# Folding the inverse features of a third pair of samples in a two-layer spectral and gated kernel, with the order of work kept as a list

## The chip, the cores and the metric

One core of a Trainium2 chip runs one program. The metric is the device time of the program in microseconds: before the change 1087.72 us, the median of 3 runs (1087.59 to 1087.82). Lower is better.

## The reference, cut to what matters

Two layers of two parts each, on x of 2048 rows (sequence) by 512 columns (features), all in single precision:

```
x = x + irfft2(rfft2(layernorm(x)) * (w_r + 1j*w_i))
n = layernorm(x)
x = x + ((n @ w_gate) * (n @ w_up)) @ w_down      # 512 -> 1792 -> 512
(the same two lines once more, with the same weights)
```

## The kernel before

**Tiling.** The 2048 rows lie as 16 tiles of 128 rows and 512 columns, called samples here (index t of `xs`). The spectral part goes in three stages: per sample the feature transform and the first part of the sequence transform (`fwd`), then the rest of the sequence transform with the filter in 16 blocks of frequencies (`middle`), then back, per sample (`inv`). The gated part (`unit`, `down`) multiplies in blocks with seven products in place of eight (names gx, gy, gw, gz, gv), each single-precision operand split into a high and a low part and multiplied in three matmuls. It reads X: the normalised, transposed samples and four sums of them, high and low (tiles xA and xS).

**The inverse and its pairs.** `inv` (L718 on) takes one sample: four twiddle products with the frequency tile E into a PSUM bank (tile vp), a ScalarE copy to SBUF (vs), the feature products with the matrix `di` into a second bank (tile yi), three VectorE additions of the bank to `xs`, and the statistics of the new row for the layer norm. In each layer the first half of the sequence goes in four pairs of samples, (0, 4), (1, 5), (2, 6), (3, 7); after each, `build_x` normalises the pair, transposes it on TensorE (tile tq) and makes X. The second half (samples 8 to 15) follows while the gated part already works on the first. The first unit of the gated part reads X of the pairs (0, 4) and (1, 5) only, the next half unit that of the other two.

**Two modes of the feature products.** In mode "plain" each of the four matmuls has 256 columns, and even and odd frequencies accumulate in the bank; the three additions read the bank as it is. In mode "fold" each matmul has 128 columns, and even and odd parts stay apart in the two halves of the bank. Then ScalarE copies the second half to SBUF (tile yb), and VectorE makes difference and sum of the halves in the bank, before the same three additions:

```
        if fold:
            yb = temp("yb", "f", (128, 256))
            act(256, lambda: A.copy(yb(), yi()[:, 256:512]), [yi], [yb])
            dve(256, lambda: tt(yi()[:, 256:512], yi()[:, 0:256], yb(), ALU.subtract), [yb], [yi])
            dve(256, lambda: tt(yi()[:, 0:256], yi()[:, 0:256], yb(), ALU.add), [yb], [yi])
```

`MODES` names the mode of each of the first half's four pairs in each layer; the second half is always folded. So 12 samples are plain and 20 folded.

**The order.** The program does not issue work as it is written. `Plan.op` records 5053 operations, each with its engine, a duration from a small cost formula, a due time and what it depends on; a tile belongs to a ring of buffers or banks. `Plan.order` then decides the order of all, which is also the order in each engine's queue: due times are carried backwards through the dependences, a scheduler (`run`) takes on each engine what is ready and due first, and a list of numbers (`MOVES`) seeds changes of due times, after each of which the order is made again from that place on. The transposed pairs use ring "d", the banks vp and yi of the pairs (2, 6) and (3, 7) and of the second half ring "a" with three banks. Engine queues run in order.

Of the kernel before, what the change touches and what calls it, by code (L numbers as in the profile page):

```python
# [26 lines left out]
def consts():  # L27
# [51 lines left out]
MODES = ("plain", "plain", "plain", "fold"), ("plain", "plain", "plain", "fold")  # L79
# [6 lines left out]
MOVES = (  # L86
# [32 lines left out]
RATE = 270.0  # L119
WARM = 2  # L120
EARLY = 0
HOLD, FAR = {"DVE": 1.0, "ACT": 1.0, "POOL": 1.0}, 15.0
CLEAR = 1.5
FREE = ("a", "f", "st", "s1", "s2", "s3")
LOOK, SLACK = 0.08, 20.0
# [23 lines left out]
class Draw:  # L149


    def __init__(self, seed):
        self.at = seed * 0x9E3779B97F4A7C15 % 2 ** 64

    def part(self):
        self.at = (self.at + 0x9E3779B97F4A7C15) % 2 ** 64
        z = self.at
        z = (z ^ z >> 30) * 0xBF58476D1CE4E5B9 % 2 ** 64
        z = (z ^ z >> 27) * 0x94D049BB133111EB % 2 ** 64
        return ((z ^ z >> 31) >> 11) * 2.0 ** -53  # L160

    def one(self, of):
        return of[int(self.part() * len(of))]

    def bell(self):
        return (self.part() + self.part() + self.part() + self.part() - 2.0) * 1.7320508


class Plan:
# [6 lines left out]
    FREE = FREE  # L176
# [31 lines left out]
    def order(self, hop=0.12):  # L208

        ops = self.ops  # L210
        for o in reversed(ops):
            d = min([ops[s]["due"] for s in o["suc"]] + [1e9 if o["due"] is None else o["due"]])
            o["due"] = d - 1.1 * o["lag"] - hop - 0.3 * (o["e"] == "PE")
        self.kinds = [(o["e"], *(t.name for t in o["tiles"])) for o in ops]
        out, marks = self.run([], [])
        for n in MOVES:
            out, marks = self.run(out, *self.move(n, out, marks)[:1])
        return out

    def move(self, n, out, marks):  # L220


        ops, draw = self.ops, Draw(n)
        end = max(o["end"] for o in out)
        lo, span = -20.0 + draw.part() * (end + 10.0), draw.one((10.0, 20.0, 40.0, 80.0, 160.0))
        share, jit, way = draw.one((0.0, 0.25, 0.5, 1.0)), draw.one((0.0, 0.0, 2.0, 5.0)), draw.part()
        inside = [o for o in ops if lo < o["start"] < lo + span]
        if way < 0.4 and inside:
            kind, by = self.kinds[draw.one(inside)["i"]], 8.0 * draw.bell()
            for o in inside:  # L230
                if self.kinds[o["i"]] == kind:
                    o["due"] += by
        elif way < 0.7 and inside:
            for _ in range(1 + int(3.0 * draw.part())):
                draw.one(inside)["due"] += 8.0 * draw.bell()
        elif inside:
            self.latest(out, end)
            shifts = sorted(o["late"] - o["due"] for o in inside)
            shift = shifts[len(shifts) // 2]
            for o in inside:  # L240
                o["due"] += share * (o["late"] - shift - o["due"]) + jit * draw.bell()
        return [m for m in marks if m[1] < lo - 15.0], lo + span

    def latest(self, out, end):
        ops = self.ops
        nxt, two = {}, None
        for o in reversed(out):
            long = o["end"] - o["start"]
            late = end - long
            for s in o["suc"]:  # L250
                late = min(late, ops[s]["late"] - (0.0 if ops[s]["next_to"] is o else long))
            if o["e"] in nxt:
                late = min(late, nxt[o["e"]] - o["pitch"])
            if o["two"]:
                if two is not None:
                    late = min(late, two - o["pitch"])
                two = late
            for t in o["tiles"]:
                if t in self.after:
                    late = min(late, self.after[t]["late"] - long)  # L260
            nxt[o["e"]] = late
            o["late"] = late

    @staticmethod
    def after_(p, o):
# [3 lines left out]
        if p["e"] != o["e"] or p["kb"]:  # L269
            return p["end"]  # L270
        return p["start"] + p["pitch"] if o["e"] == "PE" else p["end"] - 0.1

    def run(self, best, marks, pace=None, look=LOOK, hop=0.12, slack=SLACK):

        ops = self.ops
        marks = list(marks)
        m, rings, free, bus, port, after = 0, {}, {"SP": 0.75, "AQ": 0.75, "PE": 0.9, "POOL": 0.5}, 0.75, 0.0, {}
        if marks:
            m, _, rings, free, bus, port, after = marks[-1]
# [28 lines left out]
        while len(out) < len(ops):  # L308
            nexts = []
# [967 lines left out]
```

## Time and profile before

| | before |
|---|---|
| median of 3 runs | 1087.72 us |
| the profiled execution | 1087.75 us |
| its span, first to last instruction | 1086.0 us |
| TensorE busy | 1072.3 us (99%) |
| VectorE busy | 841.1 us (77%) |
| ScalarE busy | 457.7 us (42%) |
| GpSimd busy | 731.8 us (67%) |
| granted TensorE clock | 1.00 |

The profile records one execution. Busy time is the time in which an engine had an instruction under way; the ends of matmuls are modelled, and the times of consecutive ones overlap, so the distance from start to start says what one takes. All recorded work of the kernel's helpers has one line (L411), so instructions are told apart by their tiles. A granted clock of 1.00 is TensorE's full clock.

### The profile page before, as it was taken

The numbers are of one execution on the slowest core, as the hardware profiler recorded it, in microseconds if no ns is written. First come the engines' busy times: TensorE is split into PE (matmuls) and PEld (weight loads), VectorE is DVE, ScalarE is ACT, GpSimd is POOL, SyncE is SP. The second block draws the span as 40 slices with busy tenths as digits, with TensorE's granted clock in tenths as the row PEclk, the third lists the DMA queues.
The fourth block names the chain that finished last, engine by engine and source line by source line (L and its number), as shares of the span: only waits on it lengthen the run. The fifth ranks groups of instructions, "written<-read, shape, count | busy, mean of one in ns | idle before, by whom it ended". The sixth has DMA issues, their size and how long they took to land.

```text
span 1086.0 us, 18629 instructions
## 1 busy us (share of the span) xinstructions
PE 1072.3 (99%) x6500; PEld 923.2 (85%) x6500; DVE 841.1 (77%) x1684; ACT 457.7 (42%) x1045; POOL 731.8 (67%) x940
## 2 busy tenths in 40 slices
PE   8999999999999999999999999999999999999998
PEld 6748988888899988888996489889989998888887
DVE  8597877777877875766897979777897876677778
ACT  6787643344542323323347775223442521223231
POOL 7396799978898666456674527466656984667771
PEclk9999999999999999999999999999999999999999
DMA  7665267556563457454454312655456256556542
GB/s 282 234 213 175 64 223 242 199 204 203 214 223 117 166 182 235 155 165 147 136 199 151 136 54 103 207 168 180 155 175 204 69 175 242 186 184 203 194 137 78
DMA packets 50301, 189.49 MB, mean 174 GB/s; under 512 B 5280, under 2 KB 19104, under 8 KB 39200
## 3 DMA queue, kind: packets, MB, share of 16 engines
q0 software_dynamic: 16128, 102.77, 28.8%
q1 hardware_dynamic: 33792, 85.01, 22.2%
q8 instruction: 52, 0.85, 0.3%
q10 hardware_dynamic: 288, 0.52, 0.1%
q14 instruction: 41, 0.34, 0.1%
HBM read 145.56 MB, written 42.73 MB: 173 GB/s over the span
## 4 chain that ended last, share of the span: by engine, by line
PE 89%; DVE 5%; issue 2%; ACT 2%; POOL 1%; DMA 0%; DVEq 0%; POOLq 0%; ACTq 0%
PE gx L411 14%; PE gz L411 14%; PE db L411 7%; PE gw L411 7%; PE gv L411 7%; PE gy L411 7%; PE ex L411 5%; PE ez L411 5%; PE yi L411 3%; PE ey L411 3%; PE ew L411 3%; PE ev L411 3%; PE sp L411 2%; PE dp L411 2%; PE vp L411 2%
## 5 line engine op out<-in xcount | busy, mean ns | idle before, releaser
L411 PE MATMUL gx<-xA,wt 128*128 128x512 f32 (+1 forms) x852 | 180.8, 347 | 0.0
L411 PEld LDWEIGHTS gx<-xA,wt 128*128 128x128 f32 x852 | 136.9, 190 | 17.2 <-ACT s L411 0.2
L411 DVE TENSOR_TENSOR q<-gy,s 128x512 f32<-128x512 f32 (+1 forms) x71 | 41.1, 578 | 73.4 <-PE gy L411 55.9
L411 ACT CAST sf<-q 128x256 fp32r<-128x256 f32 x99 | 40.2, 406 | 136.5 <-DVE q L411 84.0
L411 POOL TENSOR_TENSOR sf<-q,sf 128x256 fp32r<-128x256 f32 x99 | 73.6, 745 | 31.8 <-ACT sf L411 28.1
L411 DVE TENSOR_TENSOR xs<-xs,db 128x512 f32<-128x512 f32 x128 | 85.6, 683 | 11.4 <-PE db L411 11.0
L411 PE MATMUL db<-wd,h 128*128 128x512 f32 x336 | 91.1, 395 | 0.0
L411 POOL DMA_DIRECT2D wt<-gu x72 | 40.3, 560 | 74.7 <-PE gz L411 48.1
L411 PE MATMUL gz<-xA,wt 128*128 128x512 f32 (+1 forms) x426 | 90.1, 347 | 0.0
L411 PE MATMUL gw<-xS,wt 128*128 128x512 f32 (+1 forms) x426 | 90.0, 347 | 0.0
L411 PE MATMUL gv<-xS,wt 128*128 128x512 f32 (+1 forms) x426 | 90.0, 347 | 0.0
L411 PE MATMUL gz<-xS,wt 128*128 128x512 f32 (+1 forms) x426 | 89.8, 346 | 0.0
L411 PE MATMUL gy<-xS,wt 128*128 128x512 f32 (+1 forms) x426 | 89.7, 346 | 0.0
L411 POOL TENSOR_TENSOR sf<-cc,sf 128x256 fp32r<-128x256 f32 x99 | 73.2, 740 | 21.1 <-ACT sf L411 20.7
L411 PEld LDWEIGHTS gz<-xA,wt 128*128 128x128 f32 x426 | 69.1, 189 | 9.4
L411 PEld LDWEIGHTS gw<-xS,wt 128*128 128x128 f32 x426 | 68.8, 189 | 9.3 <-issue 0.3
L411 PEld LDWEIGHTS gy<-xS,wt 128*128 128x128 f32 x426 | 68.7, 190 | 9.0 <-issue 0.3
L411 PEld LDWEIGHTS gz<-xS,wt 128*128 128x128 f32 x426 | 68.8, 190 | 8.9
L411 PEld LDWEIGHTS gv<-xS,wt 128*128 128x128 f32 x426 | 68.5, 190 | 8.9 <-issue 0.3
L411 ACT COPY s<-gx 128x512 f32<-128x512 f32 (+1 forms) x71 | 35.3, 497 | 92.7 <-PE gx L411 80.7
L411 PEld LDWEIGHTS db<-wd,h 128*128 128x128 f32 x336 | 60.3, 189 | 10.3
L411 ACT CAST sf<-cc 128x256 fp32r<-128x256 f32 x99 | 40.1, 405 | 66.4 <-PE ez L411 22.3
(171 smaller groups left out, 2667.1 us busy)
## 6 DMA issues: line engine op xcount, KB each, us to landing
wt<-gu POOLq DMA_DIRECT2D x36, 1024.0 KB, 5.3
wt<-gu POOLq DMA_DIRECT2D x36, 768.0 KB, 4.7
bf<-dn POOLq DMA_DIRECT2D x20, 1024.0 KB, 5.5
bf<-dn POOLq DMA_DIRECT2D x20, 768.0 KB, 4.6
gu<-wt SPq DMA_DIRECT2D x14, 1024.0 KB, 6.9
gu<-wt SPq DMA_DIRECT2D x14, 768.0 KB, 3.5
wq<-in_wf_dram SPq DMA_DIRECT2D x10, 1024.0 KB, 6.1
rg<-in_wb_dram SPq DMA_DIRECT2D x14, 512.0 KB, 4.8
```

Source lines behind the costliest of these rows:

```text
L411: ins = f(*args, **kw)
```

## The change

In both layers the pair (2, 6) goes from "plain" to "fold", as (3, 7) already is: in four samples the four feature matmuls have 128 in place of 256 columns, and one ScalarE copy and two VectorE operations are added. That makes 12 operations more, 5065 in all.

The search for an order no longer runs when the program is built: `Draw`, `move`, `latest` and `run` go, and `order` takes the operations as a list of their numbers, `ORDER`, says, keeping the bookkeeping of buffers and banks. The list was searched anew, so the order differs in many places over the whole program, not only where pairs are folded.

```diff
-MODES = ("plain", "plain", "plain", "fold"), ("plain", "plain", "plain", "fold")
+MODES = ("plain", "plain", "fold", "fold"), ("plain", "plain", "fold", "fold")
...
+ORDER = (
...
+    572, 321, 583, 530, 681, 505, 323, 519, 324, 531, 584, 325, 326, 585, 586, 506, 327, 573, 587, 328, 532, 588, 590,
+    533, 589, 329, 534, 518, 591, 535, 574, 695, 623, 696, 520, 575, 638, 538, 536, 576, 697, 637, 577, 521, 537, 578,
+    592, 539, 593, 639, 597, 598, 682, 599, 594, 595, 683, 602, 596, 522, 698, 600, 523, 603, 524, 684, 601, 525, 699,
+    330, 640, 606, 700, 604, 526, 624, 701, 607, 540, 625, 613, 331, 641, 609, 541, 608, 642, 545, 626, 546, 547, 610,
+    542, 615, 543, 544, 550, 685, 643, 616, 702, 548, 551, 611, 644, 686, 862, 849, 554, 703, 612, 617, 687, 619, 555,
+    618, 605, 688, 621, 561, 704, 620, 689, 553, 627, 705, 562, 645, 500, 690, 511, 501, 502, 706, 708, 622, 741, 646,
+    514, 628, 883, 614, 707, 515, 629, 549, 691, 647, 1040, 512, 709, 516, 630, 863, 552, 556, 513, 650, 850, 557, 648,
+    565, 559, 851, 649, 896, 566, 864, 631, 563, 742, 852, 651, 564, 692, 853, 558, 743, 632, 567, 560, 744, 865, 693,
+    568, 633, 710, 747, 634, 711, 854, 745, 884, 635, 746, 885, 652, 715, 653, 748, 716, 717, 657, 886, 658, 659, 750,
+    720, 654, 655, 749, 866, 656, 662, 712, 751, 721, 713, 752, 917, 714, 753, 660, 855, 856, 718, 768, 857, 1093, 769,
...
+    3135, 3070, 3136, 3081, 3137, 3138, 3139, 3082, 3083, 3244, 3140, 3071, 3245, 3084, 3231, 3072, 3141, 3085, 3246,
+    3232, 3422, 3087, 3073, 3086, 3074, 3247, 3469, 3142, 3075, 3233, 3088, 3189, 3146, 3143, 3089, 3147, 3148, 3248,
+    3144, 3090, 3145, 3173, 3249, 3151, 3094, 3174, 3091, 3190, 3095, 3096, 3152, 3250, 3149, 3191, 3456, 3092, 3192,
+    3175, 3150, 3093, 3155, 3251, 3156, 3234, 3193, 3157, 3158, 3153, 3252, 3194, 3235, 3159, 3164, 3253, 3154, 3236,
+    3160, 3176, 3168, 3195, 3254, 3162, 3161, 3436, 3166, 3237, 3177, 3437, 3165, 3163, 3255, 3099, 3238, 3167, 3170,
+    3178, 3100, 3097, 3239, 3169, 3179, 3103, 3240, 3098, 3171, 3196, 3180, 3423, 3104, 3101, 3424, 3181, 3110, 3105,
+    3102, 3182, 3425, 3111, 3106, 3197, 3457, 3108, 3256, 3292, 3107, 3112, 3199, 3293, 3198, 3257, 3258, 3113, 3109,
+    3183, 3114, 3426, 3438, 3115, 3200, 3116, 3184, 3241, 3295, 3201, 3202, 3117, 3427, 3439, 3242, 3206, 3203, 3294,
...
-        self.kinds = [(o["e"], *(t.name for t in o["tiles"])) for o in ops]
-        out, marks = self.run([], [])
-        for n in MOVES:
-            out, marks = self.run(out, *self.move(n, out, marks)[:1])
-        return out
...
+        for o in (ops[n] for n in ORDER):
+            e = o["e"]
+            at = max([self.after_(ops[p], o) for p in o["pre"]] + [free.get(e, 0.75), port if o["two"] else 0.0])
...
                     if len(q) == self.RINGS.get(t.ring, 1):
                         old = min((u for u in q if not u.left), key=lambda u: u.freed)
-                        after[old] = o
+                        at = max(at, old.freed)
                         q.remove(old)
```

The numbers count the operations in the order in which the program makes them. Layer 0, the first lines of the list shown: 698, 640, 685 and 627 are the feature products of samples 7, 6, 3 and 2; 641 to 643 and 628 to 630 are copy, difference and sum that folding adds for samples 6 and 2; 603 and 601, 551 and 549 are the transposes of the pairs (1, 5) and (0, 4); 741 and 742 are the first two products of the gated part, gw and gx; 850 and 851, 863 and 864 are the twiddle products of samples 8 and 12, and 853 the feature products of sample 8; 705 to 707 and 647 to 649 are ScalarE's statistics of samples 7 and 6. Layer 1, the second lines: 3189 are the feature products of sample 6; 3292 and 3293 are gw and gx, and 3457 is one of the twiddle products of sample 9, the other of which comes later.

## Rows read from the trace of the kernel before

**Rows 1.** Busy time of each engine, its share of the span, and instructions.
```profile
PE 1072.3 (99%) x6500; PEld 923.2 (85%) x6500; DVE 841.1 (77%) x1684; ACT 457.7 (42%) x1045; POOL 731.8 (67%) x940
```

**Rows 2.** Windows: length, busy us (instructions) of each engine, clock, DMA share, GB/s.
```profile
0.00:50.00 50.00, 45.33 (x335) 35.41 (x336) 33.37 (x107) 33.45 (x87) 24.91 (x39) 1.00 0.76 271
50.00:86.00 36.00, 34.89 (x92) 15.64 (x91) 35.07 (x63) 28.93 (x54) 32.80 (x32) 1.00 0.56 196
...
92.00:116.00 24.00, 22.41 (x162) 20.71 (x162) 20.96 (x73) 21.53 (x61) 11.76 (x16) 1.00 0.41 149
98.00:110.00 12.00, 10.41 (x73) 9.22 (x73) 11.33 (x36) 11.41 (x32) 6.03 (x9) 1.00 0.63 229
140.00:260.00 120.00, 120.00 (x569) 100.63 (x568) 91.34 (x172) 47.80 (x94) 104.81 (x110) 1.00 0.66 228
...
630.00:654.00 24.00, 22.90 (x164) 21.18 (x162) 21.38 (x73) 20.71 (x59) 8.55 (x12) 1.00 0.13 39
636.00:648.00 12.00, 10.90 (x74) 9.57 (x73) 11.12 (x35) 10.34 (x29) 4.60 (x7) 1.00 0.08 23
980.00:1086.00 106.00, 101.89 (x610) 90.24 (x608) 80.31 (x129) 27.10 (x63) 61.30 (x86) 1.00 0.47 155
```

**Rows 3.** Chain that ended last: start us, us, engine, tile, instructions.
```profile
0.75 3.82 DMA xs<-in_x_dram
...
91.56 1.73 PE yi L411 x8
...
105.84 1.23 ACT sq L411 x4
...
107.76 0.71 ACT sq L411 x2
...
114.19 0.89 PE yi L411 x8
...
647.07 2.38 PE vp L411 x20
...
1080.67 1.28 DVE xs L411 x2
```

**Rows 4.** Groups by shape: count | busy us, mean ns | idle before.
```profile
L411 DVE TENSOR_TENSOR xs<-xs,yi 128x256 f32<-128x256 f32 x64 | 25.3, 414 | 0.3
...
L411 DVE TENSOR_TENSOR xs<-xs,yi 128x512 f32<-128x512 f32 x32 | 21.9, 683 | 9.7 <-PE yi L411 9.3
...
L411 DVE TENSOR_TENSOR yi<-yi,yb 128x256 f32<-128x256 f32 x40 | 17.0, 428 | 3.9 <-ACT yb L411 3.2
...
L411 ACT COPY yb<-yi 128x256 f32<-128x256 f32 x20 | 7.5, 377 | 8.0 <-PE yi L411 5.1 <-POOL u L411 1.2 <-POOL h L411 0.9
...
L411 ACT CAST xS<-sx 128x256 fp32r<-128x256 f32 x16 | 6.2, 408 | 0.9 <-DVE sx L411 0.7 <-POOL sx L411 0.2
```

**Rows 5.** Who waited for tile yb: us, times.
```profile
  DVE yi L411: 3.2, 4
```

**Rows 6.** TensorE's waits, whole span: us in total, times, longest us.
```profile
PE tq L411 <- ACT xn L411: 1.6, 2, 1.2
...
PE yi L411 <- ACT vs L411: 1.1, 2, 0.7
```

**Rows 7.** Timeline of TensorE in layer 0: start, us, tile, shape, count, idle before.
```profile
106.80 2.04 PE L411 MATMUL vp<-tw,E 128*128 128x128 f32 x16
108.67 0.60 PE L411 MATMUL tq<-ident,xn 128*128 128x128 f32 x4
109.71 1.16 PE L411 MATMUL yi<-di,vs 128*128 128x128 f32 x8 [0.43 <-ACT vs L411]
110.62 0.96 PE L411 MATMUL gw<-xS,wt 128*128 128x256 f32 x6
```

**Rows 8.** Timeline of GpSimd in layer 0.
```profile
106.85 3.51 POOL L411 TENSOR_TENSOR xS<-sx,xS 128x256 fp32r<-128x256 f32 x5
```

**Rows 9.** Timeline of TensorE in layer 1.
```profile
649.21 0.96 PE L411 MATMUL gx<-xA,wt 128*128 128x256 f32 x6
```

More of the change, by code (lines that the diff above doesn't have):

```diff
@@ L85 @@
 ON_POOL = range(16), range(16)
-MOVES = (
[32 rows of a table removed]
+ORDER = (
[257 rows of a table added]
 RATE = 270.0
@@ L121 @@
 EARLY = 0
-HOLD, FAR = {"DVE": 1.0, "ACT": 1.0, "POOL": 1.0}, 15.0
 CLEAR = 1.5
-FREE = ("a", "f", "st", "s1", "s2", "s3")
-LOOK, SLACK = 0.08, 20.0
 SLOTS = 5
@@ L146, in __call__ @@
         return self.tile
[L149 to L166, printed above, removed]
 class Plan:
@@ L174 @@
              **{f"{r}{p}": n for p in range(4) for r, n in (("s", SLOTS),)}}
-    FREE = FREE
     def __init__(self):
@@ L208, in order @@
     def order(self, hop=0.12):
-        ops = self.ops
+        ops, out, rings, free, bus, port = self.ops, [], {}, {}, 0.75, 0.0
         for o in reversed(ops):
@@ L213, in order @@
             o["due"] = d - 1.1 * o["lag"] - hop - 0.3 * (o["e"] == "PE")
-        self.kinds = [(o["e"], *(t.name for t in o["tiles"])) for o in ops]
-        out, marks = self.run([], [])
-        for n in MOVES:
-            out, marks = self.run(out, *self.move(n, out, marks)[:1])
-        return out
[L220 to L262, printed above, removed]
+        for o in ops:
+            for t in o["tiles"]:
+                t.left, t.slot, t.freed = t.users, None, 0.0
@@ new lines, in order @@
+        for o in (ops[n] for n in ORDER):
+            e = o["e"]
+            at = max([self.after_(ops[p], o) for p in o["pre"]] + [free.get(e, 0.75), port if o["two"] else 0.0])
+            if e == "SP":
+                at = max(at, o["due"] - o["ahead"])
+            for t in o["tiles"]:
+                if t.slot is None:
+                    t.slot = True
+                    q = rings.setdefault(t.ring, [])
+                    t.index = len(q)
+                    if len(q) == self.RINGS.get(t.ring, 1):
+                        old = min((u for u in q if not u.left), key=lambda u: u.freed)
+                        at = max(at, old.freed)
+                        q.remove(old)
+                        t.index = old.index
+                    q.append(t)
+            o["start"] = at
+            free[e] = at + o["pitch"]
+            if o["two"]:
+                port = at + o["pitch"]
+            if o["kb"]:
+                bus = max(bus, at) + o["kb"] / RATE
+                o["end"] = max(at + o["lag"], bus + 2.3)
+            else:
+                o["end"] = at + o["lag"] + hop + 0.3 * (e == "PE")
+            for t in o["tiles"]:
+                t.left -= 1
+                t.freed = max(t.freed, o["end"])
+            out.append(o)
@@ L271, in after_ @@
         return p["start"] + p["pitch"] if o["e"] == "PE" else p["end"] - 0.1
[L273 to L279, printed above, removed]
-        rings, free, after, out = {g: list(q) for g, q in rings.items()}, dict(free), dict(after), best[:m]
-        done, mark = sum(o["e"] == "PE" for o in out), marks[-1][1] if marks else 0.0
-        ready, turn = {}, {}
-        for o in ops:
-            o["n"], o["out"] = len(o["pre"]), False
-            for t in o["tiles"]:
-                t.left, t.slot, t.freed, t.due = t.users, None, 0.0, None
-        for o in out:
-            o["out"] = True
-            for s in o["suc"]:
-                ops[s]["n"] -= 1
-            for t in o["tiles"]:
-                t.left -= 1
-                t.slot, t.freed = True, max(t.freed, o["end"])
-        for o in sorted(ops, key=lambda o: (o["due"], o["i"])):
-            for t in o["tiles"]:
-                if t.due is None:
-                    t.due = o["due"]
-                    if t.slot is None:
-                        turn.setdefault(t.ring, []).append(t)
-        def enter(o):
-            o["at"] = max([self.after_(ops[p], o) for p in o["pre"]], default=0.0)
-            ready.setdefault(o["e"], []).append(o)
-        for o in ops:
-            if not o["n"] and not o["out"]:
-                enter(o)
-        while len(out) < len(ops):
-            nexts = []
-            for e, cand in sorted(ready.items(), key=lambda r: free.get(r[0], 0.0)):
-                if nexts and free.get(e, 0.0) > min(a for a, _ in nexts) + look:
-                    break
-                can = []
-                for o in cand:
-                    at = max(o["at"], free.get(e, 0.0), port if o["two"] else 0.0)
-                    if e == "SP":
-                        at = max(at, o["due"] - o["ahead"])
-                    want, early = {}, False
-                    for t in o["tiles"]:
-                        if t.slot is None:
-                            early = early or t.due > turn[t.ring][0].due + (slack if t.ring in self.FREE else 0.0)
-                            want[t.ring] = want.get(t.ring, 0) + 1
-                    if early:
-                        continue
-                    for g, n in want.items():
-                        when = sorted(t.freed for t in rings.get(g, ()) if not t.left)
-                        n -= self.RINGS.get(g, 1) - len(rings.get(g, ()))
-                        at = max(at, 1e9 if n > len(when) else when[n - 1] if n > 0 else 0.0)
-                    if at < 1e9:
-                        can.append((at, o))
-                if can:
-                    first = min(a for a, _ in can)
-                    take = min(((a, o) for a, o in can if a <= first + look), key=lambda c: (c[1]["due"], c[1]["i"]))
-                    if e in HOLD:
-                        soon = [(a, o) for a, o in can if a < take[0] + HOLD[e] * take[1]["pitch"] and o["due"] < take[1]["due"] - FAR]
-                        take = min(soon, key=lambda c: (c[1]["due"], c[1]["i"]), default=take)
-                    nexts.append(take)
-            if not nexts:
-                raise AssertionError([(o["e"], o["i"], [t.ring for t in o["tiles"]]) for c in ready.values() for o in c][:40])
-            first = min(a for a, _ in nexts)
-            if first > mark + 20.0:
-                mark = first
-                marks.append((len(out), first, {g: list(q) for g, q in rings.items()}, dict(free), bus, port, dict(after)))
-            at, o = min((c for c in nexts if c[0] <= first + look), key=lambda c: (c[1]["due"], c[1]["i"]))
-            if o["e"] == "PE":
-                assert not pace or at < pace[done]
-                done += 1
-            ready[o["e"]].remove(o)
-            for t in o["tiles"]:
-                if t.slot is None:
-                    t.slot = True
-                    q = rings.setdefault(t.ring, [])
-                    t.index = len(q)
-                    if len(q) == self.RINGS.get(t.ring, 1):
-                        old = min((u for u in q if not u.left), key=lambda u: u.freed)
-                        after[old] = o
-                        q.remove(old)
-                        t.index = old.index
-                    q.append(t)
-                    turn[t.ring].remove(t)
-            o["start"] = at
-            free[o["e"]] = at + o["pitch"]
-            if o["two"]:
-                port = at + o["pitch"]
-            if o["kb"]:
-                bus = max(bus, at) + o["kb"] / RATE
-                o["end"] = max(at + o["lag"], bus + 2.3)
-            else:
-                o["end"] = at + o["lag"] + hop + 0.3 * (o["e"] == "PE")
-            for t in o["tiles"]:
-                t.left -= 1
-                t.freed = max(t.freed, o["end"])
-            out.append(o)
-            for s in o["suc"]:
-                ops[s]["n"] -= 1
-                if not ops[s]["n"]:
-                    enter(ops[s])
-        self.after, self.marks = after, marks
-        return out, marks
```

271 rows, old and new, of tables (MOVES, ORDER) are left out of this document.

## Prediction, made before the changed kernel was run

> **What bounds the kernel now.** I read the profile in five views: engine totals, windows by stage, the chain that ended last, TensorE's waits, and timelines of the two places that the change touches.
>
> TensorE is busy 1072.3 of 1086.0 us [rows 1]: 13.7 us of idleness in all. The windows place it [rows 2]: 4.67 us in the first 50 us, 1.11 in 50 to 86, 1.59 in 92 to 116, 1.10 in 630 to 654, 4.11 in the last 106, about 1.1 over the rest. In the long gated stage (140 to 260 stands for the others) it is never idle. So whatever TensorE no longer has to do shortens the program, but only where it would not then stand still instead. The granted clock is 1.00 in every window, TensorE's upper level of 2.4 GHz, so the clock is no term here.
>
> The change sits in the two stretches where that condition is in doubt. In 98 to 110 us TensorE is busy 10.41 of 12 us, VectorE 11.33 and ScalarE 11.41; in 636 to 648 it is 10.90, 11.12 and 10.34 [rows 2]. The chain there runs over ScalarE's statistics [rows 3] and comes back to TensorE at 109.71 us, where TensorE stood still for ScalarE's copy [rows 7]. TensorE's waits for a normalised row (1.2 and 0.4 us) and for that copy (0.7 and 0.4) all lie in these two stretches [rows 6]. Locally, VectorE and ScalarE set the pace, and TensorE is kept going with work of the second half of the sequence, pulled forward.
>
> The profiled execution took 1087.75 us, 1.75 outside its span; the median of the runs is 1087.72. I sum on the profiled one and take the difference over to the median as it is.
>
> **The fold on TensorE.** The plain features of a sample are eight instructions in 1.73 us, the folded ones eight in 0.89 [rows 3]. Four samples change (6 and 2, in each layer): 4 x 0.84 = 3.36 us less TensorE work. This is the only large term with a sure sign.
>
> **What the fold adds.** Per sample one ScalarE copy of 377 ns and two VectorE operations of 428 ns [rows 4]: per layer 0.75 us on ScalarE and 4 x 0.428 = 1.71 on VectorE. What would hide them is free time on these engines. In 92 to 116 VectorE has 24 - 20.96 = 3.04 us free, ScalarE 2.47; in 630 to 654 it is 2.62 and 3.29 [rows 2]. By these rows they fit. But in the inner 12 us VectorE has only 0.67 and 0.88 us free, ScalarE 0.59 and 1.66, and the added operations have to run in there, ahead of or among the operations that build X for the first product. Cost from both sides: nothing if the free time takes all, 2 x 1.71 = +3.42 us if all stands on the path to X.
>
> The fold also adds a wait: VectorE's difference needs ScalarE's copy, and behind it on VectorE queue the additions to xs and the small scale operations that ScalarE's normalisation waits for. The existing 20 folded samples paid 3.2 us in 4 waits for such a copy [rows 5]: 0.8 us when it happens, so 0 to 3.2 us for four. I take nothing of its own for it, since it falls into the same VectorE time as the term above. The bank of the features stays occupied longer by copy and two operations, 0.38 + 0.86, less the 0.84 that the features are shorter: 0.4 us a sample, 0 to 1.6 in all. I take 0, because the list lets other samples' work come between.
>
> **The order.** The list can be read directly, since it numbers the operations as the program makes them. In layer 0 the first product gw (741) now stands ahead of the twiddle products of samples 8 and 12 (850, 851, 863, 864), the features of sample 8 (853) and the second transpose of pair 0 (549). Before, all of these ran ahead of it: 108.67 - 106.80 = 1.87, 110.62 - 109.71 = 0.91, and 0.60 us [rows 7]. With 1.68 us saved, TensorE comes to gw 5.06 us earlier, if nothing else holds it. What holds it is X. The last low part that gw reads is the fourth of five GpSimd operations that begin at 106.85 and take 3.51 us, so it was ready near 106.85 + 4 x 0.70 = 109.65 [rows 8]. On ScalarE statistics of samples 7 and 6 (1.23 and 0.71 us in the chain, [rows 3]) go behind the cast that this part needs, against one copy and one cast more ahead of it (0.38 and 0.41, [rows 4]): 1.94 - 0.79 = 1.15 us earlier. On VectorE four operations of 256 columns and one of 512 leave (4 x 0.42 + 0.68), two fold operations enter (0.86): 1.5 us earlier. The smaller holds: X near 108.5, so gw near 108.5 instead of 110.62, while 1.87 + 0.91 + 0.60 = 3.38 us of moved work is still to be done: 3.4 - 2.1 = +1.3 us. The other end is that X follows TensorE fully: -1.68. I take +0.4: the moved work can stand in waits behind gw, where X for gx is not ready yet, but the row on X is the nearer one.
>
> In layer 1 TensorE reached gx (649.21) without a wait [rows 9], after five twiddle products of the second half, 2.38 us in the chain [rows 3]. Now one of the five, some 0.48 us, comes behind gx, so TensorE is there 2.16 us earlier. VectorE has 1.71 us more ahead of X and the list moves little of its work back. Ends: -1.68 if free time takes all; +1.71 if X comes that much later. I take -0.4: VectorE's 2.62 us free in this stretch exceed the addition, but only 0.88 of them lie in the inner 12 us.
>
> The rest of the list differs from the old order by a few places nearly everywhere. In the gated stages there is no idle time to win. In the head (4.67) most is the first load, 3.82 us in the chain [rows 3]. The tail's 4.11 us end in a VectorE chain, its last pair of additions 1.28 us [rows 3], and the list leaves the last five VectorE operations as they were. Between -2.0 and +1.0; I take -0.7, half of the idle time in 50 to 86 and a little of the tail.
>
> **Sum:** +0.4 - 0.4 - 0.7 = -0.7 us; the saving of 3.36 is inside the first two terms. 1087.72 - 0.7 = 1087.0 us.
>
> A rule of the Trainium skill bears on this: "Perfetto Trace Analysis", section "Identifying the Most-Contended Engine", says that matmul busy time misleads, that weight-load time should be read instead, and that the engine with the highest occupancy is the one to relieve. In 98 to 110 us weight loads take 9.22 of 12 us, below VectorE and ScalarE [rows 2], so by that rule this change relieves the wrong engine in its own stretch; it is the slower rival below. The rows bear it out for the inner 12 us, not for the program, where TensorE stands above both.
>
> **Rivals.**
> (a) X follows. VectorE's free time takes the additions, TensorE waits no longer than before, and all of the 3.36 us is kept. For it: both stretches have more free time on VectorE than is added. Against: the inner windows. Time: 1087.72 - 3.36 - 0.7 = 1083.7 us; with a third lost, 1084.8.
> (b) VectorE becomes the bound; the slower side. Eight added operations stand ahead of X, TensorE's saving turns into waiting for the first product, and the time grows by up to 3.42 us. It decides from the point where the additions exceed the 0.67 and 0.88 us of the inner windows, which leaves 3.42 - 1.55 = +1.9 at least. For it: the inner windows and the chain over ScalarE. Against: the list defers the statistics of samples 6 and 7. Time: +3.42 - 0.7 gives 1090.4 us; from 1089.6 on.
> (c) The new order decides and the fold does not matter: head, tail and the two spectral stages move by more than 2 us. It needs idle time that the windows show only at both ends; its times lie within the range and I give it no case of its own.
>
> **How the numbers follow.** About 0.2% (2.2 us) is what a measurement of this kernel can tell from no change: 1085.5 to 1089.9. My forecast, most of the saving given back as waits, 0.47, with its own range 1085.6 to 1088.9. Rival (a) 0.35: a real removal on the engine that bounds the program, and my hand count of X may be late by more than 1 us. Rival (b) 0.18. Faster 0.35, same 0.47, slower 0.18. Range: 1083.9, where most of (a) is inside, to 1089.9, where the lighter half of (b) ends; both tails together leave out about 0.2.
>
> **What would show it.** Right: features of 128 columns 192 instead of 160, TensorE busy some 3 us less, and its idle time in the two stretches larger by 2 to 4 us, in front of gw in layer 0 and gx in layer 1. The difference's wait for the copy would show as VectorE idle before the fold. For (a): idle in 92 to 116 and 630 to 654 stays near 1.59 and 1.10. For (b): VectorE over 95% from the first addition to the first product and the gated stage starting later than 110.6 and 649.2 us. I am wrong if the time is outside 1085.5 to 1089.9, or if the head or tail moves by more than 2 us.

## The result, and the profile after

The changed kernel takes 1091.17 us (median of 7 runs, 1090.04 to 1092.71) against 1087.82 us for the kernel before beside it (7 runs, 1087.26 to 1088.80): ratio 1.003, 95% interval 1.0019 to 1.0041. It is 3.3 us slower. I had forecast 1087.0, and 1083.9 to 1089.9 as the range.

The profiled execution took 1090.87 us, its span 1089.1. Engine totals, in the columns of [rows 1]:

```profile
PE 1070.4 (98%) x6500; PEld 921.9 (85%) x6500; DVE 846.2 (78%) x1692; ACT 458.7 (42%) x1049; POOL 732.6 (67%) x940
```

TensorE is busy 1.9 us less and VectorE 5.1 us more. So TensorE stands idle 18.7 us instead of 13.7. The windows, in the columns of [rows 2]; the first, 92 to 116, 98 to 110, 630 to 654 and 636 to 648 answer to rows there:

```profile
0.00:50.00 50.00, 46.23 (x336) 35.32 (x337) 32.15 (x108) 34.56 (x87) 24.63 (x39) 1.00 0.75 262
92.00:116.00 24.00, 20.59 (x162) 19.31 (x161) 22.04 (x72) 21.79 (x63) 11.01 (x15) 1.00 0.50 176
98.00:110.00 12.00, 8.89 (x71) 8.01 (x69) 11.19 (x35) 11.48 (x35) 8.13 (x12) 1.00 0.54 183
630.00:654.00 24.00, 21.15 (x152) 19.38 (x151) 21.97 (x70) 19.67 (x58) 8.42 (x12) 1.00 0.13 38
636.00:648.00 12.00, 10.06 (x79) 9.10 (x77) 11.60 (x41) 11.40 (x33) 4.93 (x7) 1.00 0.12 37
```

TensorE's idle time in 92 to 116 is 24 - 20.59 = 3.41 us (1.59 before), in 630 to 654 it is 2.85 (1.10 before): together +3.57, against 3.36 us of work saved. So the two stretches gain next to nothing, as the prediction had it; how much of the +3.57 is the fold's is told by e2 below. The features by shape, in the columns of [rows 4], and TensorE's waits as in [rows 6]:

```profile
L488 PE MATMUL yi<-di,vs 128*128 128x128 f32 x192 | 25.6, 277 | 4.0 <-DVE xs L488 3.3 <-ACT vs L488 0.7
L488 PE MATMUL yi<-di,vs 128*128 128x256 f32 x64 | 14.6, 379 | 0.0
```
```profile
PE yi L488 <- DVE xs L488: 3.3, 2, 2.1
...
PE ez L488 <- DVE xs L488: 0.9, 1, 0.9
...
PE ew L488 <- DVE xs L488: 0.2, 1, 0.2
```

192 features have 128 columns, as announced. Two kinds of wait are new: a features step for VectorE's additions to xs (2.10 and 1.21 us), since they hold the bank of ring "a" that it needs; and ez and ew for such additions. The first sits here, in TensorE's timeline of layer 0 (columns as in [rows 7]):

```profile
101.37 1.16 PE L488 MATMUL yi<-di,vs 128*128 128x128 f32 x8 [0.68 <-ACT vs L488]
102.39 0.66 PE L488 MATMUL tq<-ident,xn 128*128 128x128 f32 x4
105.14 1.16 PE L488 MATMUL yi<-di,vs 128*128 128x128 f32 x8 [2.10 <-DVE xs L488]
106.05 0.96 PE L488 MATMUL gw<-xS,wt 128*128 128x256 f32 x6
107.12 0.66 PE L488 MATMUL tq<-ident,xn 128*128 128x128 f32 x4
107.61 2.05 PE L488 MATMUL vp<-tw,E 128*128 128x128 f32 x16
109.42 0.36 PE L488 MATMUL gx<-xA,wt 128*128 128x256 f32 x1
110.29 0.86 PE L488 MATMUL gx<-xA,wt 128*128 128x256 f32 x5 [0.51 <-DVE xA L488]
...
651.05 0.96 PE L488 MATMUL gw<-xS,wt 128*128 128x256 f32 x6
```

gw starts at 106.05 instead of 110.62 [rows 7], sooner than the 108.5 that I had worked out for X, but the stall came before it and the moved work (transpose and twiddle products) still follows. In layer 1 (last row) the first product starts at 651.05 instead of 649.21 [rows 9].

That leaves most of the 3.3 us outside the two stretches, where the prediction had expected a small gain. Part of it shows as idle time at the end of layer 0's gated stage with the forward transform of layer 1 (550 to 600 us, called the handover below), and part in the gated stage of layer 1. Before, then after:

```profile
550.00:570.00 20.00, 20.00 (x165) 18.85 (x163) 19.05 (x48) 10.09 (x26) 15.10 (x22) 1.00 0.60 218
570.00:600.00 30.00, 29.16 (x182) 20.00 (x181) 22.73 (x55) 21.74 (x50) 15.68 (x19) 1.00 0.47 169
700.00:980.00 280.00, 280.00 (x1792) 254.68 (x1792) 215.60 (x387) 91.72 (x207) 183.35 (x256) 1.00 0.53 172
```
```profile
550.00:570.00 20.00, 19.80 (x163) 18.51 (x161) 17.97 (x42) 8.20 (x22) 12.78 (x18) 1.00 0.61 219
570.00:600.00 30.00, 28.30 (x187) 20.61 (x186) 23.19 (x56) 22.05 (x53) 15.16 (x19) 1.00 0.43 146
700.00:980.00 280.00, 279.23 (x1781) 253.39 (x1780) 217.69 (x388) 91.02 (x205) 183.06 (x254) 1.00 0.53 173
```

TensorE is idle 1.90 us in the handover instead of 0.84, and 0.77 instead of 0 in 700 to 980.

### The profile page after: what moved, and what is told of

The parts are those of the page before. It is cut to its first block, busy times and chain, and to the rows that moved or that the text cites. A ratio compares the mean times of both kernels' runs of the same rounds, so it can differ in the third digit from the quotient of the medians.

```text
span 1089.1 us, 18628 instructions
## 1 busy us (share of the span) xinstructions
PE 1070.4 (98%) x6500; PEld 921.9 (85%) x6500; DVE 846.2 (78%) x1692; ACT 458.7 (42%) x1049; POOL 732.6 (67%) x940
## 4 chain that ended last, share of the span: by engine, by line
PE 91%; DVE 3%; ACT 2%; DMA 2%; issue 1%; POOL 0%; POOLq 0%; DVEq 0%
PE gx L488 14%; PE gz L488 14%; PE db L488 8%; PE gy L488 7%; PE gv L488 7%; PE gw L488 7%; PE ez L488 5%; PE ex L488 5%; PE yp L488 3%; PE dp L488 3%; PE sp L488 3%; PE yi L488 3%; PE ev L488 3%; PE ey L488 2%; PE ew L488 2%; PE zp L488 2%
## 5 line engine op out<-in xcount | busy, mean ns | idle before, releaser
L488 PEld LDWEIGHTS gx<-xA,wt 128*128 128x128 f32 x852 | 137.9, 190 | 18.7 <-DVE xA L488 0.9
L488 POOL TENSOR_TENSOR sf<-q,sf 128x256 fp32r<-128x256 f32 x94 | 70.1, 746 | 36.0 <-ACT sf L488 34.8
```

Of the source, the lines that this page charges most:

```text
L488: ins = f(*args, **kw)
```

## The experiments

The theories. BANK: the wait for the bank in ring "a" is the cost. VECTOR: VectorE's added work is the cost, whichever buffer shows it. ORDER: the newly searched order is slower by itself, with or without the fold; PLACE says its loss has places that add up, SPREAD that it hasn't. CLOCK: TensorE's granted clock falls behind a stall. "Old order" is the kernel before's, written as a list; every median is given against the median of the kernel before, measured beside it, with the 95% interval of the ratio.

**e1, e2: order and fold taken apart.** e1 is the old order with the fold, e2 the new order without it:

```diff
-MODES = ("plain", "plain", "fold", "fold"), ("plain", "plain", "fold", "fold")
+MODES = ("plain", "plain", "plain", "fold"), ("plain", "plain", "plain", "fold")   # e2
 ORDER = (
...   # e1: old order, per sample copy + difference + sum put in; e2: new order less these twelve
```

> The order of the kernel before, kept as a list, with the third pair folded in both layers: each copy stands behind its features, each difference and sum ahead of the first addition; everything else is as before. Theory BANK (the features of samples 6 and 2 wait for a bank of ring a, which VectorE's longer additions hold; 2.10 and 1.21 us in the profile after): the fold itself costs, so this is no faster than before, 1087 to 1090. Theory VECTOR (the added 3.4 us of VectorE work are served ahead of what TensorE needs next, whichever buffer shows it): the same 1087 to 1090, the idle of 92 to 116 and 630 to 654 about 3 us above before. Theory ORDER (the fold gives its 3.4 us or nearly, and the newly searched order loses about 6 elsewhere): 1084 to 1086.

> The order of the changed kernel with its twelve added instructions taken out, and the third pair's features plain as before. Theory ORDER: the order is what is slower, so this is 1091 or, with the TensorE work back, up to 1094. Theories BANK and VECTOR: the order costs what the idle outside the two stretches shows, about 1.4 us, so 1088 to 1090.

Measured: e1 1093.29 (+5.6; ratio 1.0040 to 1.0065), e2 1091.19 (+3.5; 1.0020 to 1.0045). e2 is the changed kernel's time without the fold in it: on the new order the fold nets 0.0 us, to within some 1.8 us by the two intervals, and the order alone is 3.5 us slower. ORDER holds for the changed kernel. The two stretches in e2's profile, and its wait for the bank, as in [rows 2] and [rows 6]:

```profile
92.00:116.00 24.00, 21.37 (x156) 19.88 (x155) 20.52 (x66) 20.94 (x58) 10.72 (x15) 1.00 0.50 176
630.00:654.00 24.00, 22.52 (x151) 20.59 (x151) 20.88 (x64) 18.88 (x55) 8.27 (x12) 1.00 0.13 39
PE yi L488 <- DVE xs L488: 1.8, 1, 1.8
```

TensorE is idle 2.63 + 1.48 = 4.11 us there, so 1.42 of the +3.57 us come with the order and 2.15 with the fold, and most of the longer wait for the bank is there without the fold.

On the old order the fold costs far more than any theory had for it: the ranges ended at 1090. The twelve operations were put into that order by hand, each copy right behind its features, and VectorE's queue then stands still for the copy, in e1's timeline of layer 0:

```profile
104.78 0.90 DVE L489 TENSOR_TENSOR yi<-yi,yb 128x256 f32<-128x256 f32 x2 [1.45 <-ACT yb L489]
```

In all VectorE waits for the copy 4.9 us in 6 cases in e1, against 3.2 in 4 before and 0.9 in 2 in the changed kernel. An order searched from the old one for the fold was not run, so e1's price is that of this placement.

**e3, e4: the new order, the added work out, or the bank wait out.**

```diff
-        if fold:
+        if fold and t not in (2, 6):     # e3
             yb = temp("yb", "f", (128, 256))
-... if k < 2 else ("a", "a"),
+... if k < 2 else ("a", {7: "y", 3: "x"}.get(t, "a")),     # e4
```

> The changed kernel with the third pair's features folded but its copy, difference and sum left out (the added features of samples 2, 3's partner 6, of both layers are then not put together; what is left out is four copies, four differences, four sums). Theory VECTOR: the work was the price, the time falls by 2.5 to 4 us to 1087 to 1088.5. Theory BANK: the additions start earlier, so the wait for the bank goes as well, the same 1087 to 1088.5. Theory ORDER: the added work hardly matters, 1090 to 1091.

> The changed kernel with the same order and work, but the features of samples 7 and 3 (the fourth pair) in the banks y and x, which lie idle there, so that ring a has a free bank when the features of 6 and 2 come up. Theory BANK: the waits of 2.10 and 1.21 us go and the time falls by 2 to 3.3 us, to 1088 to 1089. Theory VECTOR: TensorE starts the features earlier and waits as long a little later, for the transposes or the first products; time within 1 us of 1091. Theory ORDER: as VECTOR.

(In e3 the samples meant are 2 and 6.) Measured: e3 1089.31 (+1.6; 1.0004 to 1.0021), 1.9 under the changed kernel and between the ranges of VECTOR and ORDER; e4 1091.70 (+4.0; 1.0025 to 1.0047). In e4 TensorE's timeline shows the bank wait gone and others in its place:

```profile
102.30 0.66 PE L489 MATMUL tq<-ident,xn 128*128 128x128 f32 x4 [0.80 <-ACT xn L489]
102.79 1.06 PE L489 MATMUL yi<-di,vs 128*128 128x128 f32 x8
105.02 0.38 PE L489 MATMUL gw<-xS,wt 128*128 128x256 f32 x1 [1.18 <-ACT xS L489]
106.01 0.85 PE L489 MATMUL gw<-xS,wt 128*128 128x256 f32 x5 [0.60 <-POOL xS L489]
```

The features of sample 2 no longer wait (102.79); TensorE waits 0.80 us for a normalised row ahead of them and 1.18 + 0.60 us for X behind them. In the two stretches TensorE is busy 21.24 and 20.76 of 24 us, so idle 6.0 us, against 6.3 in the changed kernel. BANK falls by these rows; VECTOR's "waits as long a little later" is what they show. The time alone would not settle it, since in e4's profile the granted clock of 92 to 116 is 0.93, and 1.00 in the changed kernel's. e3's gain of 1.9 us, under its expected 2.5 to 4, is the price of the added ScalarE and VectorE work on the new order, and the change's profit on TensorE there is as large (e3 is also 1.9 under e2).

**e5, e6, e7: the two halves of the fold, on the old order.** e5 issues the third pair's folded features twice, so only the added work is left; e6 leaves the added work out; e7 unfolds the fourth pair too.

```diff
-            for i in range(4):
+            for i in (*range(4), *(range(4) if t in (2, 6) else ())):     # e5
```

> The kernel of e1_old_order_fold with each folded features matmul of the third pair issued twice (the same result), so that TensorE's 3.4 us come back and only the added work of ScalarE and VectorE is left as the change. Theory VECTOR: in the two stretches TensorE waits for VectorE anyway, so the 3.4 us fall into its idle time: not slower than e1's 1093.3. Theory CLOCK (e1's profile has TensorE at half clock in 106 to 112 and 650 to 654, right behind its idle time, some 3.4 us of lost work; with TensorE busier the clock stays): faster than e1 although TensorE does more, 1089.5 to 1091.5. If TensorE's saving was real in e1: 1096 to 1097.

> The order of the kernel before, the third pair's features folded, but without the copies, differences and sums (the added features of samples 2 and 6 are then not put together): TensorE's saving alone. Theory VECTOR: without VectorE's added work the saving shows, at most 3.4 us, 1085 to 1087. Theory CLOCK: VectorE's old work already sets the pace, the saved time becomes idle and the clock falls behind it: 1087.5 to 1090. If the saving counts in full: 1084.3.

> The order of the kernel before with the fourth pair's features plain as well (four copies, four differences and four sums fewer, TensorE +3.4 us). Theory VECTOR: before has 2.7 us of idle TensorE time in the two stretches, and VectorE's additions end earlier, so at most 1 to 2.5 us are lost or nothing: 1087.5 to 1090. If TensorE is what counts there: 1091.

Measured: e5 1094.15 (+6.35; 1.0046 to 1.0071), e6 1087.89 (+0.1; 0.9990 to 1.0008), e7 1089.89 (+2.1; 1.0010 to 1.0027). For e5 both VECTOR and CLOCK had expected no more than 1093.3, and the count in full 1096: all miss. e6 lies in CLOCK's range, e7 in VECTOR's. The windows tell why; 92 to 116 and 630 to 654 in e1, e5 and e6, columns as in [rows 2], the clock third from the end:

```profile
92.00:116.00 24.00, 19.22 (x136) 18.23 (x135) 19.75 (x64) 19.84 (x56) 11.24 (x15) 0.93 0.42 149
630.00:654.00 24.00, 20.57 (x132) 18.94 (x131) 19.92 (x60) 17.31 (x47) 5.49 (x8) 0.93 0.15 46
```
```profile
92.00:116.00 24.00, 20.65 (x144) 19.95 (x144) 18.49 (x58) 18.30 (x51) 9.75 (x14) 0.86 0.41 148
630.00:654.00 24.00, 21.49 (x153) 19.89 (x151) 19.02 (x58) 17.31 (x47) 5.02 (x7) 1.00 0.17 49
```
```profile
92.00:116.00 24.00, 21.99 (x162) 21.13 (x161) 20.93 (x73) 21.50 (x61) 11.56 (x16) 0.93 0.40 149
630.00:654.00 24.00, 21.50 (x161) 20.14 (x161) 21.34 (x72) 20.20 (x59) 8.55 (x12) 1.00 0.13 39
```

A granted clock below 1.00 over 24 us is lost work that busy time hides: (1 - 0.93) x 24 = 1.7 us. With it, three terms from each profile (TensorE's work, its idle time in the two stretches against before's 1.59 + 1.10, the lost work) come near the times, all in us:

| | work | idle | clock | sum | measured |
|---|---|---|---|---|---|
| e1 fold | -3.4 | +5.5 | +3.4 | +5.5 | +5.6 |
| e5 added work only | 0 | +3.2 | +3.4 | +6.5 | +6.35 |
| e6 TensorE's saving only | -3.4 | +1.8 | +1.7 | +0.1 | +0.1 |
| e7 nothing folded | +3.4 | -0.8 | 0 | +2.6 | +2.1 |
| e9 (below) | +5.0 | -0.4 | 0 | +4.7 | +4.8 |

The sums are a reading and not a measurement: each takes the windows of one execution, and they leave out the first 50 us, where e1's clock is 0.97 and its TensorE 1.1 us less idle. For e6 the clock's term is too large: three of its eleven executions have a mean clock of 1.00 and take 1086.96 to 1087.73, the other eight (0.997 and 0.998) 1087.47 to 1088.25, medians only 0.4 apart. So where the clock stays up, most of its 1.7 us seems to be waited instead.

So on the old order TensorE's saving is worth nothing that can be told even when VectorE pays nothing for it (e6), and the added work, 3.4 us on VectorE, costs 6.3 (e5). Near half of that price fits the wait for the copy: in e5's profile VectorE waits for it 6.7 us in 6 cases, 3.5 more than before. The fourth pair's fold, which before has already, is worth 2.1 (e7): the first fold pays, the second doesn't. What fits, and was not tested, is that VectorE had room for the first (busy 8.63 of 12 us in 98 to 110 in e7) and has little for the second (11.33 before).

**e9: the stalls filled.** Thirteen matmuls that nobody reads, where TensorE waited in e1:

```diff
+    def keep_busy(wz, m):
+        for _ in range(m):
+            TE.matmul(wz()[:, 0:384], ident, midt, start=True, stop=True, skip_group_check=True)
```

> The kernel of e1_old_order_fold (1093.3) with thirteen matmuls of 128x384 that nobody reads, put ahead of the instructions for which TensorE waited in its profile: four and four in layer 0 (waits of 2.00 and 2.25 us), one, three and one in layer 1 (0.54, 1.54, 0.67). Theory CLOCK: TensorE stays at the full granted clock behind them, and the lost work of about 1.7 us in 106 to 112 and 1.7 us in 650 to 654 comes back: 1089 to 1091.5, faster although TensorE does 5 us more. Rival VECTOR ALONE: VectorE's and ScalarE's results come when they come and the clock costs nothing that they don't hide: 1093 to 1095.

Measured: 1092.56 (1092.33 to 1092.67), 0.7 under e1 (1092.61 to 1093.46), not the 2 to 4 us of the expectation, and under the rival's 1093 to 1095 as well. TensorE's windows of 2 us in e1 and then in e9 (length, busy us (instructions), clock, DMA share, GB/s):

```profile
106.00:108.00 2.00, 0.55 (x2) 0.88 1.05 435
108.00:110.00 2.00, 2.00 (x12) 0.50 0.73 307
110.00:112.00 2.00, 2.00 (x15) 0.77 0.00 0
...
650.00:652.00 2.00, 2.00 (x11) 0.56 0.00 0
652.00:654.00 2.00, 2.00 (x13) 0.59 0.16 48
```
```profile
106.00:108.00 2.00, 2.00 (x10) 1.00 1.03 432
108.00:110.00 2.00, 2.00 (x20) 1.00 0.50 209
110.00:112.00 2.00, 1.57 (x14) 1.00 0.03 8
...
650.00:652.00 2.00, 1.40 (x13) 1.00 0.05 12
652.00:654.00 2.00, 2.00 (x19) 1.00 0.30 93
```

In e1 the clock is at 0.50 (1.2 GHz) behind the stalls; in e9 it stays at 1.00 (2.4 GHz). The gain is small because the fillers were too long. Eight records of them run from 102.05 to the next step at 104.63, so 26 take 26/8 x 2.58 = 8.4 us, while the idle time fell by only 8.2 - 2.3 = 5.9. 8.4 - 5.9 less 3.4 of clock is -0.9, near the -0.7. More TensorE work made the kernel a little faster, as CLOCK says; the number in the expectation rested on the fillers' wrong length.

**e8, e10 to e14: where the new order loses.** All plain, spliced from both orders:

```diff
 ORDER = (
...   # e8: new to place 450, then old; e10: new to 800; e13: new to 2250
...   # e11: new in 2250 to 2880, else old; e12: old to 2880, then new; e14: old in 2250 to 2880, else new
```

Behind a seam the second order goes on with what has not been issued yet.

> Plain third pair; the order of the changed kernel up to the end of the filter stage of layer 0 (the first 450 places of the list), then that of the kernel before. In the profiles the new order reaches the first inverse twiddle after the filter 0.5 to 1.0 us sooner (84.5 to 85.0 us against 85.5) and loses later, in the stretches and at the handover near 570 us. Theory ORDER-PLACE: the head's gain stays and the losses go: 1086.7 to 1087.2. Rival: the second half of the head's gain is lost again in the first stretch, which waits for ScalarE and VectorE: 1087.7.

> Plain third pair; the changed kernel's order for the first 800 places (to behind the stretch of layer 0), then that of the kernel before. Theory PLACE (the new order's loss of 3.4 us in e2 is the sum of its idle time: stretch 0 about 1.0, handover 570 about 1.1, stretch 1 about 0.9, the rest in the gated stage of layer 1): head -0.4 and stretch +1.0, so 1088 to 1089. Rival: the loss lies in this part whole: 1091.

> Plain third pair; the order of the kernel before, with the changed kernel's order in places 2250 to 2880 (the end of layer 0's gated stage and the forward transform of layer 1, where TensorE waits 0.20 and 0.86 us for VectorE's xs near 567 and 572 us in the new order and not in the old). Theory PLACE: 1088.5 to 1089. Rival: the waits there are made up at the filter stage, which VectorE bounds: 1087.7.

> Plain third pair; the order of the kernel before for the first 2880 places, then the changed kernel's (filter of layer 1, its stretch, its gated stage and the end). Theory PLACE: +0.9 for the stretch and up to 1 for waits on loads in the gated stage (0.4 us twice in the profile of the changed kernel, none before): 1088.5 to 1089.8, with a wider spread than before's. Rival: the loss of 3.4 us lies here whole, since only here the two orders' executions differ in spread: 1091.

> Plain third pair; the changed kernel's order for the first 2250 places (all of layer 0 but the end of its gated stage), then that of the kernel before; at that place both have issued the same operations. Theory PLACE (the parts of e2's 3.4 us add up: handover 1.8, from filter 1 on 0.7, so 0.9 is left for layer 0): 1088.3 to 1089.2. Rival SPREAD (no one place: loads that come late by chance of phase, in any mixture with the new beginning): 1090 to 1091 with a spread over 2 us, as e10.

> Plain third pair; the changed kernel's order but for places 2250 to 2880 (the handover near 570 us), which follow the kernel before. Theory PLACE: e2 less the handover's 1.8, 1089.0 to 1089.8. Rival SPREAD: 1090.5 to 1091.5, no better than e2 by more than 0.7.

Measured: e8 1087.34 (-0.5; 0.9987 to 1.0005, no difference shown), e10 1091.22 (+3.5; 1.0019 to 1.0044), e11 1089.57 (+1.8; 1.0006 to 1.0024), e12 1088.42 (+0.7; 1.0000 to 1.0018), e13 1089.01 (+1.2; 1.0007 to 1.0025), e14 1089.85 (+2.0; 1.0017 to 1.0034). e10, in its rival's range, misled: its profile has waits of 0.39 and 0.55 us near 177 and 195 us, behind the seam, and one of 0.88 us for a load near 864, that neither before's profile nor e2's has. Cut at place 2250, where both orders have issued the same set but for one operation, layer 0 costs 1.2; with the handover's 1.8 (e11, 0.6 above PLACE's range) and the rest's 0.7 (e12, 0.1 below it) that is 3.7 against e2's 3.5. The sum fits PLACE, but each piece has an interval of some 1 us to either side. e14, 1.3 under e2, is 0.05 above PLACE's range and 0.65 below SPREAD's; seven of its executions take 1089.63 to 1089.94 and four 1091.60 to 1091.82, so its median hangs on how many fall in either group. The largest piece by the sum is the handover. TensorE there in e11:

```profile
567.00 0.98 PE L488 MATMUL ew<-bf,sf 128*128 128x256 f32 x6 [0.20 <-DVE xs L488]
...
572.00 0.95 PE L488 MATMUL ez<-bf,sf 128*128 128x256 f32 x6 [0.85 <-DVE xs L488]
...
587.47 1.16 PE L488 MATMUL dp<-df,fs 128*128 128x128 f32 x8 [0.47 <-ACT E L488]
```

0.20 + 0.85 + 0.47 = 1.5 us of waits that the old order doesn't have; the first two stand in the changed kernel's profile too. In the windows before, this part had next to no idle time (0.84 us in 50): the prediction looked for idle time to win, found little here, and did not ask what could be lost.

**e15, e16: the fold on better orders.** e15 is the changed kernel with the old order at the handover (e14 with the fold), e16 is e13 with the fold in layer 0 alone.

> The changed kernel itself (third pair folded in both layers) with the same old handover as e14. If the fold nets nothing on the new order, as the changed kernel against e2 says: the same as e14, within 0.7 us. Theory PLACE: 1089 to 1090; rival SPREAD: 1090.5 to 1091.5.

> e13 with the third pair folded in layer 0 only, by the changed kernel's order there. My prediction priced the fold of layer 0 with its order at +0.4. If layer 0's fold nets nothing: as e13, within 0.7 us. If VectorE's work costs there: 1 us or more above e13.

Measured: e15 1091.04 (+3.2; 1.0021 to 1.0044, between 1089.35 and 1092.79), e16 1088.73 (+0.9; 1.0003 to 1.0021). Layer 0's fold nets -0.3 against e13, nothing that can be told. e15 lies in SPREAD's range and not in PLACE's, only 0.1 under the changed kernel: there the old handover did not bring the 1.8 us back. It is 1.2 above e14, and its interval overlaps with e14's: whether layer 1's fold costs something on this order stays open, as does why executions of the full new order differ by over 2 us with the clock at 1.00. So it is shown that the new order costs 3.5 us; where it loses them is shown only in part.

## Why the prediction was wrong

The step that failed is the last term of the sum, "The rest of the list ... Between -2.0 and +1.0; I take -0.7". It measured about +3.1 in the changed kernel: the two stretches, order and fold together, account for +0.2 of the 3.3 us in the profile. In e2, without the fold, it is about +2.1: 3.5 less the 1.42 us that the order adds to the idle time of the stretches. Both are above the upper end, for which the prediction gives no reason; it asks only where idle time could be won. An order can also lose where there is next to none: the handover had TensorE full or nearly so, and results that come later there became waits (e11). For the same reason rival (c) was wrongly dismissed with "It needs idle time that the windows show only at both ends". Its first half, that the order decides and the fold does not matter, is what happened; its places, head and tail, did not move by 2 us (idle 3.77 for 4.67 us in the first 50), and its time was not within the range.

Point by point:
- *The fold's 3.36 us on TensorE*: right: 192 features of 128 columns, and the two shapes together busy 25.6 + 14.6 us, 3.5 less than before's 21.3 + 22.4.
- *Layer 0 +0.4, layer 1 -0.4*: near in size. Idle time rose by 1.82 and 1.75 us against 1.68 saved in each: +0.14 and +0.07. But 1.04 and 0.38 of the rise stand in e2 without the fold, so less of the saving was eaten by the fold's own work than the prediction had it, and part of the agreement is luck. That the fold nets nothing is also what e2 against the changed kernel, 0.0, and e16 against e13, -0.3, say within their intervals.
- *The bank held longer, taken as 0*: the bank was waited for (3.3 us), outside my bound of 1.6. The reason given, that other samples' work comes between, failed; the price of 0 came out all the same, since in e4 other waits took its place.
- *The wait for the copy, taken as 0*: right on the new order, not on the old (e1, e5). Who waited for tile yb in the changed kernel, now for all 24 copies, against 3.2 us in 4 cases for 20 [rows 5]:

```profile
  DVE yi L488: 0.9, 2
```

- *X near 108.5, gw there*: gw came at 106.05 without a wait, so the hand count of X was at least 2.4 us late; the stall that I put in front of gw stands in front of the last features.
- *Rival (a)*: did not happen. On the new order the fold nets nothing (e2), and even without the added work 1.9 of the 3.36 us are kept (e3 against e2); on the old order none (e6).
- *Rival (b)*: its first sign came: from the first difference of a folded sample to the first product VectorE was busy 7.17 of 7.35 us in layer 0 (98.70 to 106.05) and 10.96 of 10.99 in layer 1 (640.06 to 651.05). Of its second sign, only layer 1's gated stage began later. Its time, 1090.4, is close by luck: its mechanism is not what made the changed kernel slow, since its price was 1.9 us on the new order (e3), TensorE's saving paid for it, and e2 is as slow without it. On the old order the price was 6.3 us (e5). Its two bounds also don't go together: 1089.6 leaves out the -0.7 that 1090.4 contains.
- *"so the clock is no term here"*: true of the changed kernel's two stretches in its profile, but not of e1, e3, e4, e5, e6 and e15, in whose profiles the clock is halved behind idle time in one of them or both.

The rule that I had weighed, of the Trainium skill, "Perfetto Trace Analysis", section "Identifying the Most-Contended Engine", that one should relieve the engine with the highest occupancy, fits e6 in its stretch: VectorE and ScalarE were the fullest there (10.99 and 11.41 of 12 us in 98 to 110, weight loads 9.66), and relieving TensorE alone gave +0.1 us. It does not fit the new order as well: in e2 ScalarE is fullest there (10.65, weight loads 8.69), and relieving TensorE alone brought 1.9 us (e3). That section says nothing on the order, which decided.

## What to carry to other kernels

A searched order is a change of its own, to be priced by its losses: ask in the full stages what each moved step makes late, not only where idle time could be won; and measure order and edit apart, since these two experiments (e1, e2) told more here than the whole profile. Work taken from TensorE in a stretch where other engines are as full can be worth nothing (e6) or half of itself (1.9 of 3.4 us, e3), depending on the order, and the idle time that it leaves can cost the clock as well. A wait that takes a name in the profile (the bank) is not its cause until taking it away moves the time.

## What the runs showed of the hardware

The granted clock fell to half in windows behind short stalls with work in between: in e1 after waits of 2.00 and 2.25 us with one transpose step between them. Behind 1.16 us in the kernel before it did not. The length of the waits alone doesn't tell it here: behind waits of 0.68 and 1.75 us it stayed at 1.00 in e2's profile and fell in e3's behind 0.67 and 1.75; behind one of 1.99 it fell in e6's, and behind 0.68 and 2.10 it stayed in the changed kernel's. A fall seen as 0.93 over 24 us is 1.7 us of lost work, as worked out above, and busy time does not show it: e1's TensorE is busy 1073.2 us, 0.9 more than before, with 3.4 us less work; its clock fell three times, the first in the first 50 us. What the lost work adds to the time is another matter: 0.7 us less in e9, whose clock stays up, with 8.4 us of added TensorE work, and about 0.4 us between e6's executions with and without one.
